# A hand-written instruction list with the same 848 entries in another order: attention overlapped with the first pass of a feed-forward layer

## The chip, the cores and the metric

The kernel runs on one core of one Trainium2 chip. The metric is device time in microseconds (us), the median of several runs. Matmuls run on TensorE (PE; its weight loads are PEld), and element work on VectorE (DVE), ScalarE (ACT) and GpSimd (POOL). All transfers of this kernel are issued by SyncE (SP). Each engine takes its instructions strictly in the order in which the program gives them to it, and semaphores hold an instruction until its operands are there.

## The reference

Three stages, one after the other. Batch is 2, heads are 8, the sequence is 768, the head dimension is 64.

1. Attention: each query sees the keys nearer than 16 positions, and also 24 block summaries (per block of 32 keys the elementwise maximum of the keys and the mean of the values, with log 32 added to their scores). Softmax over both sets together.
2. First feed-forward layer on the 1536 x 512 result x: `h = max(x @ w_in, 0)`, `x = (h * h) @ w_out`, with a hidden size of 2048.
3. Second layer of the same shape: a rational function of `h = x @ w_in` (a cubic over a quadratic in |h|), then `@ w_out`.

Inputs of the two layers come as 64-bit floats and are decoded on the chip.

## The kernel before, in words

Matmuls of the two layers are each done as three: a number is split into a high and a low part, and high x high, high x low and low x high are summed. The layers are run in four passes over parts of the 16 tiles of the hidden size (128 columns each). Pass 0 does tiles 0 to 4 of the first layer, in six chunks of 256 tokens: 30 steps, one for each chunk and tile. Pass 1 does the other 11 tiles, passes 2 and 3 the second layer.

Pass 0 is interwoven with the attention. The attention is cut into 24 units d (six groups of 256 queries, four pairs of heads); units 4c to 4c+3 give the tokens of chunk c. The order of all instructions of this stage is written out by hand, as one string `ORDER` of 848 entries. The program walks through it and calls a function for each entry; each engine gets its instructions in the order of the entries. A scheduler orders only what follows the list, from step 28 of pass 0 on.

An entry is a letter and a number:

- SP, transfers: `E` keys of batch 0 (a pair of heads), `q_1`, `q_0` and `Q` queries of a group, `v`, `Z` values for the block means, `N` windows of values, `J` keys of batch 1, `I` raw weights of one half tile (3 buffers, so a load waits until the decoding of the one three before has read its buffer).
- Keys: `P` (POOL) rearranges them, `t` (DVE clears two PSUM banks, PE transposes), `l` and `k` copy the two banks to SBUF, `c` (DVE) takes the block maxima and writes them for some windows, `B` for the rest.
- Block means of values: `S` (POOL) adds, `V` (PE) sums up, `u` and `w` copy out.
- A unit d of attention: `q` (PE transposes queries), `z` (ACT copies them), `s` (PE scores, 4 matmuls that the trace shows as 8), `m` (DVE adds the mask and takes the maximum, 4 instructions), `e` (ACT exponential, 4), `r` (DVE sum and reciprocal, 2), `n` (POOL scales, 4), `p` (PE transposes, 4), `b` (copies), `o` (PE times values), `x` (ACT) and `y` (DVE) split the result into its high and low part.
- Weights of one half tile: `T` (ACT), `D` (DVE, 2 instructions), `W` (ACT), `M` (POOL).
- Pass 0, step g: `h(4g)` to `h(4g+3)` (PE, 3 matmuls each, the first layer's product), `i` (ACT) and `j` (DVE) square the positive part, `G` (ACT) and `H` (POOL) split it, `Y(4g)` to `Y(4g+3)` (PE, 3 matmuls each, the second product).
- `_z0`, `_m2`, `_bw` and the like set up constants.

A star sends a copy (`l`, `k`, `B`, `u`, `w`, `b`) to DVE, without one it runs on ACT:

```python
            elif x[-1] == "*":
                parts[x[0]](int(x[1:-1]), dve)
            else:
                parts[x[0]](int(x[1:]))
```

The attention has six PSUM banks, `y0` to `y3`, `a0` and `a1`. Each user takes the one that came free earliest in the list and gives it back in the entry that reads it last:

```python
        tag = banks.pop(0)
```

From the entry `O0` on, `y0` and `y1` are kept for the sums of pass 0: the first step's `Y0` and `Y1` go into `y0`, and `Y2` and `Y3` into `y1`.

Of the kernel before, what the change touches and what calls it, by code (L numbers as in the profile page):

```python
# [16 lines left out]


ORDER = (
    "E0 _id P0 E1 q_1 t0 P1 q_0 _m0 t1 q2 q1 l0 _z0 E2 _m1 k0 k1* q3 P2 I0 E3 l1 z1 q0 c1 _pr s1 "  # L20
    "_ml z0 P3 t2 c0 _m2 k2 Q1 l2 T0 _bw s0 m0 e0 z2 c2 t3 m1 q6 l3* D0 k3 v0 B1 S0 e1 r0 n0 s2 "
    "c3 B2 W0 q4 v1 m2 S1 z3 s3 I1 q5 p0 e2 r1 V0 r2 B0 N0 m3 n1 z5 z4 s4 T1 u0 w0 p1 b0* e3 D1 "
    "M0 b1* v3 s5 n2 m4 v2 q7 p2 N1 z6 o0 o1 S2 e4 S3 I2 W1 N3 x1 r3 z7 x0 N2 b2* m5 B3* T2 n3 V1 "
    "p3 r4 s6 M1 I3 b3 Q2 u1* w1 m6 I4 y0 D2 N4 o2 N5 e5 r5 n4 T3 o3 y1 x2 h0 p4 y2 x3 I5 D3 s7 "
    "h1 W2 I6 y3 h2 n5 p5 e6 W3 q9 r6 q8 m7 M2 z9 q10 h3 z8 T4 h4 J1 J3 h5 h6 b5* b4* q11 e7 i0 "
    "D4 W4 h7 n6 i1 M3 s8 p6 m8 J2 j0 z10 o5 o4 r7 I7 s9 M4 G0 h8 x5 T5 h9 z11 x4 m9 b6* D5 H0 O0 "
    "y4 Y0 Y1 Y2 h10 n7 h11 T6 D6 j1 s10 e8 W6 W5 i2 Y3 y5 p7 J0 t5 r8 I8 N6 M6 h12 G1 H1 h13 e9 "
    "Y4 h14 m10 M5 k5* b7 n8 Y5 Y6 N7 j2 N8 h15 e10 i3 l5* r9 Y7 s11 p8 r10 N9 G2 T7 t4 T8 k4 D7 "
    "H2 Y8 D8 n10 W7 n9 W8 Z0 Y9 I9 J5 m11 Y10 M8 o6 Y11 o7 b8 o8 x6 N11 h16 h17 x7 j3 h18 J4 e11 "
    "h19 y6 y7 l4 r11 M7 c5 i4 h20 h21 h22 G3 h23 H3 p10 Y12 Y13 x8 Y14 y8 I10 i5 j4 p9 T9 b9* j5 "  # L30
    "D9 Y15 h24 G4 I11 h25 h26 h27 o9 S4 W9 M9 h28 H4 h29 i6 h30 b10* V2 h31 G5 t6 Y16 H5 Y17 j6 "
    "Y18 Y19 h32 Y20 Z1 i7 Y21 G6 k6 c4 Y22 Y23 H6 x9 Y24 Y25 Y26 T10 h33 h34 Q3 h35 n11 J7 T11 "
    "j7 u2* D10 D11 N10 i8 Y27 h36 h37 h38 j8 G7 l6* H7 W10 h39 i9 G8 M10 Y28 Y29 Y30 W11 h40 Y31 "
    "H8 j9 Y32 Y33 p11 y9 I12 q12 Y34 Y35 b11 z12 o11 x11 o10 J6 h41 I13 s12 x10 T12 y10 y11 m12 "
    "h42 h43 h44 i10 M11 h45 S5 h46 j10 G9 h47 H9 i11 N13 T13 t7 Y36 D12 G10 Y37 Y38 Y39 h48 H10 "
    "W12 e12 D13 Y40 I14 Y41 Y42 M12 q13 Q4 w2 z13 h49 h50 r12 h51 j11 k7* Y43 h52 i12 c6 G11 T14 "
    "H11 s13 W13 Y44 Y45 m13 Y46 I15 Y47 h53 e13 q14 j12 h54 h55 n12 z14 i13 G12 D14 M13 H12 h56 "
    "q15 s14 h57 l7* r13 m14 Y48 Y49 z15 Y50 N15 h58 W14 j13 e14 c7 h59 M14 p12 B4 r14 i14 G13 "
    "b12* T15 I16 n13 Y51 s15 V3 m15 e15 j14 B5* H13 u3 Y52 r15 p13 T16 Y53 Y54 b13 B7* n14 N12 "
    "B6* N14 n15 o12 p14 x12 w3* y12 o13 x13 b14* p15 Y55 b15 D15 o14 y13 x14 o15 x15 h60 Q5 y14 "  # L40
    "h61 y15 h62 h63 W15 q16 D16 M15 h64 h65 h66 i15 G14 H14 j15 h67 i16 G15 Y56 Y57 Y58 h68 j16 "
    "H15 Y59 z16 Y60 h69 h70 h71 i17 I17 Y61 Y62 G16 Y63 H16 W16 q17 s16 Y64 Y65 m16 e16 N18 Y66 "
    "z17 Y67 h72 N17 h73 j17 s17 r16 m17 q19 h74 M16 e17 h75 h76 z19 h77 i18 n16 q18 G17 p16 s19 "
    "z18 r17 m19 e19 H17 Y68 Y69 T17 Y70 Y71 j18 s18 N16 n17 h78 r19 b16 m18 q20 D17 h79 o16 e18 "
    "z20 i19 n19 G18 p19 r18 p17 W17 H18 b17* x16 s20 Y72 Y73 y16 n18 o17 x17 Y74 Y75 p18 b19 m20 "
    "b18 N19 q21 z21 y17 o19 h80 j19 x19 o18 x18 e20 M17 y19 s21 h81 y18 h82 h83 q22 i20 j20 h84 "
    "G19 h85 H19 h86 r20 h87 m21 i21 G20 H20 Y76 Y77 n20 Y78 Y79 h88 Y80 h89 Y81 h90 z22 h91 Y82 "
    "N20 j21 e21 Y83 h92 i22 h93 q23 G21 H21 N23 r21 N22 Y84 N21 Y85 h94 h95 z23 j22 Y86 i23 Y87 "
    "s22 G22 H22 p20 Y88 Y89 n21 m22 b20* Y90 e22 s23 r22 m23 Y91 h96 n22 j23 h97 h98 p21 e23 b21 "
    "h99 i24 G23 o20 r23 o21 n23 p23 x20 H23 p22 y20 Y92 x21 b23* Y93 y21 b22 j24 Y94 o22 x22 y22 "  # L50
    "Y95 o23 h100 h101 x23 y23 h102 h103 i25 j25 G24 h104 h105 h106 H24 h107 h108 i26 Y96 Y97 Y98 "
    "G25 Y99 h109 h110 h111 H25 Y100 Y101 j26 i27 Y102 j27 G26 Y103 H26 h112 Y104 h113 Y105 Y106 "
    "h114 h115 i28 h116 j28 G27 H27 h117 h118 h119 Y107 i29 j29 Y108 Y109 G28 Y110 H28 Y111 "
)


# [795 lines left out]
```

## Time and profile before

| | us |
|---|---|
| median of 3 runs (lowest, highest) | 629.76 (628.51, 630.88) |
| the profiled execution, its own time | 628.86 |
| the profiled execution, its span | 626.8 |
| last matmul of the list (`Y111`) starts | 175.73 |

The span is the time from the first to the last instruction that the profile shows; the execution's own time is 2.06 us more. The list takes the first 176 us, and the rest of the span is passes 1 to 3. A matmul's row shows its start, so that the distance between two starts is its cost in a dense stretch.

### The profile page before, as it was taken

What the parts mean: (1) busy time and instruction counts of PE and PEld (TensorE: products, weight loads), DVE (VectorE), ACT (ScalarE), POOL (GpSimd) and SP (SyncE); (2) the same over time, 40 slices, a digit from 0 to 9 for tenths busy, and PEclk for the clock granted to TensorE, in tenths of its full rate; (3) what the DMA queues carried; (4) which work ended last, traced back from release to release, by engine and by line L of the source; (5) the groups of instructions that cost most, each with busy time, mean ns of one, the idle gap of its engine ahead of it and who ended that gap; (6) DMA issues with size and microseconds to landing.
All of it is one profiled execution on the core that took longest, in us unless ns stands there. A gap on an engine that the chain in (4) does not pass through costs nothing.

```text
span 626.8 us, 9738 instructions
## 1 busy us (share of the span) xinstructions
PE 604.4 (96%) x3488; PEld 517.4 (83%) x3488; DVE 407.4 (65%) x811; ACT 402.6 (64%) x770; POOL 353.6 (56%) x363
## 2 busy tenths in 40 slices
PE   5798999999999999999999999999999999999997
PEld 5788898989988778888888888788888888888886
DVE  3988659565347674011137799988666977776673
ACT  3888558575355554122256899988878788877761
POOL 3677876444246775222277799954545764544451
PEclk9899999999999999999999999999999999999999
DMA  9978795411025553000006433410000100001011
GB/s 222 260 176 199 176 240 144 118 47 40 3 68 168 183 157 98 0 1 0 1 0 195 155 122 100 135 35 1 1 0 1 34 1 1 1 19 49 0 68 67
DMA packets 64143, 51.48 MB, mean 82 GB/s; under 512 B 39776, under 2 KB 56160, under 8 KB 64096
## 3 DMA queue, kind: packets, MB, share of 16 engines
q1 hardware_dynamic: 64096, 50.87, 29.9%
q8 instruction: 27, 0.44, 0.3%
q14 instruction: 20, 0.16, 0.1%
HBM read 47.71 MB, written 3.15 MB: 81 GB/s over the span
## 4 chain that ended last, share of the span: by engine, by line
PE 50%; DVE 7%; ACT 2%; POOL 2%; issue 1%; DMA 1%; POOLq 0%; ACTq 0%; SPq 0%; DVEq 0%
PE y L665 25%; PE h L571 25%; DVE wdec L160 2%; POOL wl L176 2%; ACT wdec L149 1%; POOL sl L641 1%; DVE acc L693 1%; DVE h L620 1%; DVE q L617 1%; DVE wdec L159 1%; DVE p L605 1%; DVE p L623 1%; DVE p L604 1%; DMA wraw<-in_moe_w_out_dram 1%; ACT sh L634 1%
## 5 line engine op out<-in xcount | busy, mean ns | idle before, releaser
L571 PE MATMUL h<-xh,wh 128*128 128x512 f32 (+1 forms) x444 | 162.4, 366 | 1.2 <-DVE r L601 0.8
L571 PE MATMUL h<-xh,wl 128*128 128x512 f32 (+1 forms) x444 | 160.1, 361 | 0.8 <-POOL wl L176 0.8
L571 PE MATMUL h<-xl,wh 128*128 128x512 f32 (+1 forms) x444 | 160.1, 361 | 0.2 <-DVE xl L539 0.2
L641 POOL TENSOR_TENSOR sl<-r,sh 128x512 fp32r<-128x512 f32 (+1 forms) x63 | 67.9, 1078 | 116.3 <-ACT sh L634 94.6
L592 POOL TENSOR_TENSOR q<-q,u 128x512 f32<-128x512 f32 x48 | 63.6, 1326 | 76.3 <-ACT q L589 74.0
L176 POOL TENSOR_TENSOR wl<-wdec,wh 128x512 fp32r<-128x512 f32 x64 | 87.5, 1374 | 25.0 <-ACT wh L171 25.0
L571 PEld LDWEIGHTS h<-xh,wh 128*128 128x128 f32 x444 | 83.6, 188 | 15.2 <-DVE p L623 1.2
L571 PEld LDWEIGHTS h<-xh,wl 128*128 128x128 f32 x444 | 83.7, 189 | 13.5 <-POOL wl L176 1.0
L571 PEld LDWEIGHTS h<-xl,wh 128*128 128x128 f32 x444 | 83.8, 189 | 12.9 <-DVE xl L539 0.4
L601 DVE TENSOR_TENSOR r<-r,h 128x512 f32<-128x512 f32 (+1 forms) x63 | 35.1, 557 | 85.5 <-ACT r L584 85.4
L665 PE MATMUL y<-sh,wh 128*128 128x512 f32 (+1 forms) x252 | 87.3, 347 | 3.4 <-DVE xl L539 1.8
L665 PE MATMUL y<-sh,wl 128*128 128x512 f32 (+1 forms) x252 | 85.1, 338 | 0.0
L665 PE MATMUL y<-sl,wh 128*128 128x512 f32 (+1 forms) x252 | 81.1, 342 | 0.6 <-POOL sl L641 0.6
L641 POOL TENSOR_TENSOR sl<-p,sh 128x512 fp32r<-128x512 f32 x48 | 64.8, 1351 | 20.4 <-ACT sh L634 17.0
L665 PE MATMUL y<-wl,sh 128*128 128x512 f32 x192 | 74.7, 389 | 0.0
L665 PE MATMUL y<-wh,sh 128*128 128x512 f32 x192 | 74.4, 389 | 0.0
L665 PE MATMUL y<-wh,sl 128*128 128x512 f32 x192 | 74.0, 389 | 0.0
L160 DVE SCALAR_TENSOR_TENSOR wdec<-wraw,wdec 128x512 int32<-128x512 int32 x64 | 68.5, 1071 | 1.7
L584 ACT ACTIVATE r<-h 128x512 f32<-128x512 f32 (+1 forms) x63 | 31.1, 494 | 47.0 <-PE h L571 25.7
L171 ACT CAST wh<-wdec 128x512 fp32r<-128x512 f32 x64 | 39.5, 620 | 33.4 <-DVE wdec L160 31.3
L634 ACT CAST sh<-r 128x512 fp32r<-128x512 f32 (+1 forms) x63 | 32.3, 513 | 39.1 <-PE y L665 38.6
L159 DVE TENSOR_SCALAR wdec<-wdec 128x512 int32<-128x512 int32 x64 | 45.9, 718 | 17.2 <-ACT wdec L149 17.0
(88 smaller groups left out, 1094.3 us busy)
## 6 DMA issues: line engine op xcount, KB each, us to landing
wraw<-in_moe_w_in_dram SPq DMA_DIRECT2D x32, 512.0 KB, 4.0
wraw<-in_moe_w_out_dram SPq DMA_DIRECT2D x32, 512.0 KB, 3.4
early<-in_v_dram SPq DMA_DIRECT2D x40, 96.0 KB, 3.8
out_dram<-acc SPq DMA_DIRECT2D x12, 256.0 KB, 2.1
acc<-in_q_dram SPq DMA_DIRECT2D x10, 256.0 KB, 6.8
early<-in_k_dram SPq DMA_DIRECT2D x4, 384.0 KB, 5.5
early<-in_v_dram SPq DMA_DIRECT2D x4, 384.0 KB, 7.8
kst<-in_k_dram SPq DMA_DIRECT2D x8, 192.0 KB, 5.3
```

Source lines behind the costliest of these rows:

```text
L149: x = nc.scalar.activation(out=f32(t), in_=f32(r[:, :, 1]), func=AF.Prelu, scale=2.0 ** -112, alpha=-(2.0 ** 32))
L159: nc.vector.tensor_single_scalar(out=t, in_=t, scalar=3, op=ALU.logical_shift_left)
L160: nc.vector.scalar_tensor_tensor(out=t, in0=low, scalar=29, in1=t, op0=ALU.logical_shift_right, op1=ALU.bitwise_or)
L171: nc.scalar.copy(out=wt[n][0][:, j], in_=f32(wdec[n, j]))
L176: nc.gpsimd.tensor_tensor(out=tl[:, j], in0=t, in1=f32(th[:, j]), op=ALU.subtract)
L571: nc.tensor.matmul(hq[g][:, 0:n], lhsT=w[:, 0, ws], rhs=x[:, part, ts], start=(part == 0 and j == 0), stop=(part == KC - 1 and j == 2),)
L584: nc.scalar.activation(out=r, in_=h, func=AF.Relu)
L592: nc.gpsimd.tensor_tensor(out=q_, in0=q_, in1=u_, op=ALU.mult)
L601: nc.vector.tensor_tensor(out=eq[g], in0=eq[g], in1=h, op=ALU.mult)
L634: nc.scalar.copy(out=sh[:, 0:n], in_=e)
L641: nc.gpsimd.tensor_tensor(out=sl[:, 0:n], in0=eq.pop(g), in1=f32(sh[:, 0:n]), op=ALU.subtract)
L665: x = nc.tensor.matmul(o, lhsT=lt, rhs=rt, start=(f == 0 and j == 0 and d * m % 512 == 0), stop=(f == FS[ps] - 1 and j == 2 and (d + 1) * ...
```

## The change

The string `ORDER` is replaced by one with the same 848 entries in another order. Nothing is added or taken away, except that 21 entries change their star: `l0`, `k6`, `B1`, `B2`, `B4`, `u0`, `w2`, `b7`, `b8` and `b13` move from ACT to DVE, and `k1`, `k5`, `k7`, `l3`, `l6`, `B5`, `u2`, `w3`, `b0`, `b12` and `b23` from DVE to ACT. No other line of the program is changed. The beginning of both lists, up to the first step of pass 0, and some of what the prediction speaks of:

```diff
 ORDER = (
-    "E0 _id P0 E1 q_1 t0 P1 q_0 _m0 t1 q2 q1 l0 _z0 E2 _m1 k0 k1* q3 P2 I0 E3 l1 z1 q0 c1 _pr s1 "
-    "_ml z0 P3 t2 c0 _m2 k2 Q1 l2 T0 _bw s0 m0 e0 z2 c2 t3 m1 q6 l3* D0 k3 v0 B1 S0 e1 r0 n0 s2 "
-    "c3 B2 W0 q4 v1 m2 S1 z3 s3 I1 q5 p0 e2 r1 V0 r2 B0 N0 m3 n1 z5 z4 s4 T1 u0 w0 p1 b0* e3 D1 "
-    "M0 b1* v3 s5 n2 m4 v2 q7 p2 N1 z6 o0 o1 S2 e4 S3 I2 W1 N3 x1 r3 z7 x0 N2 b2* m5 B3* T2 n3 V1 "
-    "p3 r4 s6 M1 I3 b3 Q2 u1* w1 m6 I4 y0 D2 N4 o2 N5 e5 r5 n4 T3 o3 y1 x2 h0 p4 y2 x3 I5 D3 s7 "
-    "h1 W2 I6 y3 h2 n5 p5 e6 W3 q9 r6 q8 m7 M2 z9 q10 h3 z8 T4 h4 J1 J3 h5 h6 b5* b4* q11 e7 i0 "
-    "D4 W4 h7 n6 i1 M3 s8 p6 m8 J2 j0 z10 o5 o4 r7 I7 s9 M4 G0 h8 x5 T5 h9 z11 x4 m9 b6* D5 H0 O0 "
-    "y4 Y0 Y1 Y2 h10 n7 h11 T6 D6 j1 s10 e8 W6 W5 i2 Y3 y5 p7 J0 t5 r8 I8 N6 M6 h12 G1 H1 h13 e9 "
...
+    "E0 _id E1 E2 P0 q_0 _m0 _pr t0 P1 k0 t1 _m1 _z0 _ml P2 l1 k1 E3 l0* q_1 _bw Q1 q0 z0 q1 c0 "
+    "t2 z1 _m2 l2 s0 P3 q3 k2 B0 c1 t3 m0 e0 q2 c2 l3 z2 r0 k3 n0 s1 q7 m1 q4 I0 v0 c3 s2 v1 q5 "
+    "N1 z3 e1 s3 v3 S0 m2 r1 p0 e2 m3 r2 T0 N0 e3 S1 B2* V0 v2 n1 z4 B1* b0 D0 q6 u0* z5 s4 w0 p1 "
+    "m4 o0 e4 r3 I1 I2 s5 z6 n2 Q2 p2 b1* B3* N2 T1 o1 m5 W0 r4 z7 x0 x1 S2 n3 s6 p3 D1 M0 I3 N3 "
+    "e5 y0 S3 I4 y1 W1 m6 n4 h0 b2* T2 e6 V1 r5 D2 q9 h1 s7 u1* q8 p4 w1 M1 b3 N5 W2 T3 z8 N4 o3 "
+    "o2 n5 x2 s8 x3 r6 D3 I5 y2 h2 y3 h3 M2 W3 q10 h4 T4 m7 D4 b4* e7 h5 n6 h6 I6 q11 W4 i0 J2 p5 "
+    "h7 b5* M3 o4 o5 z9 j0 p6 M4 i1 m8 r7 I7 G0 b6* O0 h8 x4 z10 T5 H0 h9 j1 Y0 D5 Y1 n7 T6 x5 "
+    "h10 h11 Y2 s9 N6 J3 i2 G1 W5 J1 J0 Y3 z11 D6 N7 y5 H1 m9 y4 M5 W6 Y4 Y5 Y6 I8 M6 s10 e8 t5 "
+    "N8 p7 h12 h13 T7 h14 j2 r8 m10 b7* h15 Y7 N9 k5 e10 i3 G2 Z0 t4 D7 l4 T8 I9 o6 n8 p8 H2 x6 "
+    "k4 r10 Y8 J5 D8 b8* J4 Y9 W7 Y10 W8 Y11 n10 y6 o7 M8 o8 e9 s11 h16 h17 x8 h18 I10 j3 x7 h19 "
...
 )
```

## Rows read from the trace of the kernel before

**Rows 1.** The page, busy time and share of the span: TensorE

```profile
PE 604.4 (96%) x3488; PEld 517.4 (83%) x3488; DVE 407.4 (65%) x811; ACT 402.6 (64%) x770; POOL 353.6 (56%) x363
```

**Rows 2.** Windows: stretch, length, busy us (instructions) by engine, granted clock, DMA share, GB/s

```profile
core 0: us, PE busy (x) PEld busy (x) DVE busy (x) ACT busy (x) POOL busy (x), PEclk, DMA share, GB/s
0.00:26.00 26.00, 15.76 (x90) 14.54 (x91) 15.28 (x69) 14.17 (x35) 10.77 (x26) 0.93 1.05 241
26.00:44.00 18.00, 17.00 (x184) 15.54 (x183) 16.07 (x65) 16.72 (x47) 15.61 (x27) 1.00 0.86 198
44.00:66.00 22.00, 19.15 (x216) 17.93 (x214) 19.18 (x69) 17.98 (x49) 15.70 (x25) 1.00 0.89 197
66.00:110.00 44.00, 42.37 (x396) 40.73 (x394) 31.93 (x92) 27.97 (x73) 32.10 (x47) 1.00 0.77 182
110.00:176.00 66.00, 65.00 (x644) 61.58 (x645) 32.85 (x121) 36.95 (x104) 26.95 (x53) 1.00 0.19 49
176.00:626.80 450.80, 445.08 (x1970) 367.04 (x1968) 292.05 (x398) 288.79 (x467) 252.51 (x189) 1.00 0.18 58
```

**Rows 3.** Timeline of the first 25 us: start, us, engine, line, operation, [idle before <-releaser]

```profile
4.68 1.03 POOL L303 COPY early<-early 96x1024 f32<-96x1024 f32 x1 [3.24 <-DMA early<-in_k_dram]
5.77 3.18 PE L371 MATMUL pk<-ident,early 96*128 96x96 f32 x16 [5.77 <-POOL early L303]
6.31 1.04 POOL L303 COPY early<-early 96x1024 f32<-96x1024 f32 x1 [0.60 <-DMA early<-in_k_dram]
...
8.74 1.91 PE L436 MATMUL pt<-ident,acc 128*128 128x128 f32 x8
...
9.84 1.61 ACT L444 COPY qz<-pt 64x256 f32<-64x256 f32 x4 [0.85 <-PE pt L436]
9.85 0.95 DVE L391 TENSOR_REDUCE kss<-kt 128x24 f32<-128x768 f32 x1
10.16 1.04 POOL L303 COPY early<-early 96x1024 f32<-96x1024 f32 x1 [2.27 <-DMA early<-in_k_dram]
...
11.41 2.04 PE L455 MATMUL pss<-kt,qz 128*128 128x120 f32 x8 [0.76 <-DVE kt L397]
...
13.27 1.04 POOL L303 COPY early<-early 96x1024 f32<-96x1024 f32 x1 [2.07 <-DMA early<-in_k_dram]
...
14.52 1.72 PE L455 MATMUL pss<-kt,qz 128*128 128x120 f32 x8
...
16.27 0.28 DVE L470 CUSTOM_DVE_ANT_0 pr<-pss,mask 128x120 f32<-128x120 f32 x1 [2.44 <-PE pss L455]
...
18.85 1.15 PE L371 MATMUL pk<-ident,early 96*128 96x96 f32 x8 [2.61 <-DVE pk L368]
...
23.55 1.15 PE L455 MATMUL pss<-kt,qz 128*128 128x120 f32 x8 [1.01 <-DVE mx L470]
```

**Rows 4.** Windows around the low clock, columns as in the first windows

```profile
16.00:20.00 4.00, 1.39 (x12) 1.23 (x11) 3.69 (x21) 2.38 (x7) 1.26 (x1) 0.91 1.10 283
20.00:23.00 3.00, 2.54 (x12) 2.14 (x11) 2.90 (x7) 2.97 (x9) 0.79 (x3) 0.55 1.07 250
```

**Rows 5.** Lines of the list's stretch: busy, mean ns of one | idle before

```profile
L479 ACT ACTIVATE pr<-pr,mx 128x120 f32<-128x120 f32 x96 | 30.1, 386 | 7.8 <-DVE mx L470 7.6
L470 DVE CUSTOM_DVE_ANT_0 pr<-pss,mask 128x120 f32<-128x120 f32 x96 | 21.2, 277 | 13.5 <-PE pss L455 12.2 <-POOL pr L494 1.1 <-PE ptp L504 0.2
L487 DVE TENSOR_REDUCE mx<-pr 128x4 f32<-128x484 f32 x24 | 15.6, 649 | 3.8 <-ACT pr L479 3.6
L160 DVE SCALAR_TENSOR_TENSOR wdec<-wraw,wdec 128x512 int32<-128x512 int32 x18 | 14.0, 777 | 0.6
```

**Rows 6.** Timeline at two waits of TensorE after 44 us

```profile
50.13 0.41 DVE L539 TENSOR_TENSOR xl<-pav,xh 128x256 fp32r<-128x256 f32 x1
...
50.69 0.35 PE L665 MATMUL y<-sh,wh 128*128 128x256 f32 x1 [1.75 <-DVE xl L539]
...
63.87 0.38 PE L571 MATMUL h<-xh,wl 128*128 128x256 f32 x1 [0.77 <-POOL wl L176]
```

51 rows, old and new, of the table ORDER are left out of this document.

## Prediction

> **What bounds the kernel now.** I read the page's busy times first, then windows over the list's stretch, then the timeline of the start, then the timeline at the longest waits that were left. TensorE (PE) is busy for 96% of the span [rows 1], so the time can only fall where PE waits or runs slowly. The windows say where [rows 2]: after 176 us PE is busy 445.08 of 450.80 us and runs code that the change doesn't touch; before, it has 26.00 - 15.76 = 10.24 us without work in the first 26 us, then 1.00, 2.85, 1.63 and 1.00. That is 16.7 us, and 5.77 of them come before the first keys are there and rearranged [rows 3]; 10.95 are within reach of an order. The granted clock adds to it: eight score matmuls took 2.04 us at the start and 1.15 once warm [rows 3].
>
> Within the list three kinds of stretch follow each other. Up to 16.27 us everything waits for transfers and for the first scores: the first mask instruction (`m0`) stands at 16.27, and right after it PE idles 2.61 us, because `t3` stands behind other DVE work [rows 3]. From 26 to 66 us DVE is busy 35.25 of 40 us and ACT 34.70 [rows 2]; PE's waits there are handed down from them. After 66 us DVE and ACT have a quarter or more of the time free, and PE is the bound. So a lead won early is kept if the other engines can follow, and lost if a transfer or a bank can't.
>
> **The change, part by part.** Work is not added or removed: the new list has the same entries, and 21 copies change between ACT and DVE, ten one way and eleven the other. By the lists' counts ACT gets about one copy more and DVE one less in 176 us of which both are busy less than 70%; I cost this at nothing over the stretch, at most one `k` or `l` copy (under 1 us) in the busy part, either way.
>
> *The start.* Two key loads of 384 KB reach their readers at 4.68 and 6.31 us, so 1.63 us each while the queue is full. As a check, the third comes 512 KB of queries later: 1.63 x 896/384 = 3.80, and its reader starts 3.85 us after the second [rows 3]. In the new list `E2` comes third on SP's queue and one half of the queries (`q_0`, 256 KB) fourth: landed at 7.94 and 9.03; `E3` fifth, at 10.66, in place of 13.27. POOL's `P2` runs 7.94 to 8.98. PE's order is now t0 t1 q0 q1 t2 s0: t1 is through at 8.74 as before, `q0` and `q1` wait for the queries until 9.03 and take half of the 1.91 us of four such units, to 9.99; `t2` at the low clock takes about half of the 3.18 us of the first two less the wait between them, 1.35, to 11.34; `s0` takes 16.27 - 14.52 = 1.75, to 13.1 [rows 3]. DVE has by then done `l0`, `c0`, the masks and most of `c1` (the maxima, 0.95 us each [rows 3]), and ACT `z0` (a quarter of 1.61 for each copy, done near 10.4). So `m0` starts at 13.1 in place of 16.27: **-3.2 us**. `t3` (keys at 10.66, rearranged at 11.7) follows `s0` and `q3` at 13.5 in place of 18.85, and the 2.61 us of idle PE are gone; what they cost stands in this 3.2 or in the next term, and isn't counted again.
>
> *Straight after it.* DVE's next waits in the new order are for scores: `s1` stands behind s0, q3, t3 and q2 on PE (0.48 + 1.35 + 0.48), ends near 17.1, while DVE is through with `c2` and `r0` near 16. **+1.0 us** of the lead is given back; the bounds are 0 (if the clock has risen by then, `s1` takes 1.15) and 2.
>
> *Between 26 and 44 us.* DVE idles 18 - 16.07 = 1.93 us there [rows 2]. Following the new list entry by entry I find it nearly without waits: `D0` to `D3` (0.64 + 0.78 us or a little more each, by the rows' L160 with its partner) stand later among the units, so `r6` has three of them ahead and no longer four, and the inputs of each `m` (0.28 x 4 less overlap) and `r` (0.65 and a reciprocal) are there when DVE comes [rows 5]. `e` on ACT, 0.39 x 4 less overlap [rows 5], is in the same position. The bounds are 0 and 1.93; I take three quarters, **-1.4 us**, since the first products of the layer (`h0`) still wait for `M0`, whose `W0` now stands later (ACT does `W0` after `e4` and not after `e1`). By my reading `h0` starts near 30.6 with less PE work ahead of it, and PE idles there some 1.5 us, which is priced in.
>
> *The bank of Y2.* In the old list `y1` was held by unit 4 (`o4`) when `O0` reserved it, so that `Y2` waited for `y4`, which stood behind `D5` on DVE: PE idled 1.75 us until 50.69, the last read being at 50.13 to 50.54 [rows 6]. Counting banks through the new list, `y1` is held by `q10` and given back by `z10` on ACT, which stands before `T5`; `y0` was last read by `m8`. By the time of `Y2` both are free: **-1.75 us**. If `z10` were late, 0.
>
> *The weights of h16.* The third matmul of `h16` waited 0.77 us for `M8` on POOL [rows 6]. In the new list `M8` goes before `M7` as it did, but `n9` comes after both, and `h16` stands behind o7, o8 and s11. I reckon the wait gone or halved: **-0.5 us** (0 to -0.77).
>
> *After 66 us.* PE idles 2.63 us in 110 us [rows 2]. The distances on PE between a unit's scores, its transposes and its use are about the same in both lists (units 16 to 19 have more, 21 and 22 less), so I expect the same small waits: 0, with 1.5 either way.
>
> *After the list.* The entries left are the same and the weights are equally far (18 half tiles). The rest moves up as a block; the scheduler sees another start, which I cost at 0, 1 either way.
>
> The sum is -3.2 + 1.0 - 1.4 - 1.75 - 0.5 = -5.85 us. Against the profiled execution's own 628.86 us (span 626.8 and 2.06 around it) that is 623.0. The median of the three runs, 629.76, lies 0.9 above that execution, so I put the predicted time at 623.6.
>
> **A rule weighed.** After PE had idled up to 18.85 us, the granted clock was 0.55 in 20 to 23 us [rows 4] and back at 1.00 from 26 on [rows 2]: the lower of the two levels (1.2 and 2.4 GHz) after little work. The Trainium skill (TensorE: Matmul & The Clock Gate, "HAM oscillation — how this bites in real kernels") says that a PE that keeps waiting between short bursts falls back to half speed again and again. The trace agrees for that one stretch. By the rows alone the new order takes away the long idle but leaves PE sparse between 17 and 31 us, as it runs ahead of DVE; my sum takes one such stretch in it as free, since DVE and ACT have the work there. What it would be otherwise is the second rival.
>
> **The rivals.** *Transfers become the bound.* A kernel that is 6 us ahead needs its transfers 6 us earlier. I count 14.4 MB in the new queue up to `I10`, with `J4` and `J5` for `t6` ahead of it; at the 241 GB/s of the first 26 us [rows 2] they are there at 60 us, about 4 us before I expect `t6` to want its keys. At the 197 GB/s of 44 to 66 us they come at 73 us, and nearly all of the lead goes. For it: the DMA share there is already 0.89. Against it: SP waited for free buffers in that stretch, so 197 is demand as much as limit. It gives some -1.3 us, 627.6 to 630: no change.
>
> *The clock stays low*, the case on the other side. PE is busy 17.00 us in 26 to 44 us at the full clock [rows 2]; the rows at both levels give a factor 2.04/1.15 = 1.77 [rows 3]. If the new order's sparse PE holds the low level through the like stretch, it needs 30 us there, 12 more than the 18, and the time becomes 623.6 + 12 = 635.6. Each us of that work at the low level costs 0.77 once the 1.0 us of idle is used up, so it turns the sign from about 9 us of low clock on. The skill's rule named above speaks for it; against it, the `s` at 23.55 us in the old order runs at full speed after 1.01 us of idle [rows 3].
>
> *The change does little:* the early lead is eaten by local waits in chunks 3 to 5. PE idled only 2.63 us there, but a different set of waits of 0.5 us for each of twelve units would take 6 us back: 629.6.
>
> **How the numbers follow.** No change means within 0.5% (3.1 us), about what a measurement of this kernel can tell. I give the forecast, a lead of 3.2 us or more that lasts, 0.67; the two that end without a change (transfers, later waits) 0.21 together; slower, by the clock or by a queue whose waits I read wrongly, 0.12. The lower end is 10 us under the median, 619.5, with all bounds taken well (-3.2, 0, -1.93, -1.75, -0.77, -1.5, -1); the idle of 10.95 us forbids much more. The upper end takes in the first and third rivals: 630.5.
>
> **What would show it.** In the new profile: `P2` near 8 and the third key load's reader no longer at 10.16; the first mask instruction near 13.1; no PE wait of 2.6 us before `t3`; no wait of PE on `y4` before `Y2`; the third matmul of `h16` before 59 and not at 63.87; the list's last matmul near 170. It is wrong if PE's waits for `z` or `m` grow between 17 and 31 us with the clock at 0.5 beyond 31, if SP's transfers land after their readers are ready near `t6`, or if PE's idle between 66 and 170 us is several us more than 2.63.

## The result and the profile after

The new list takes 620.00 us (median of 4, 619.52 to 620.75) against 630.32 beside it (4, 628.51 to 630.94): a ratio of 0.985, 95% interval 0.983 to 0.988. The forecast was 623.6 within 619.5 to 630.5, so the sign is right, the time lies at the low end of the range, and the gain is larger than the sum of its terms. The profiled execution took 620.43 us with a span of 618.5, so 8.3 us less of span than before. That difference is what has to be found in the trace. The other 2 us between the medians have no trace: the kernel before took 626.5 to 632.3 us over all its executions beside these runs, and the profiled one took 628.86.

The page's busy line, which answers to [rows 1]:

```profile
PE 600.2 (97%) x3488; PEld 515.6 (83%) x3488; DVE 407.6 (66%) x810; ACT 403.2 (65%) x771; POOL 356.4 (58%) x363
```

TensorE is busy for 4.2 us less with the same 3488 matmuls. Its "busy" time therefore holds more than the work, waits or matmuls at the lower clock, and that will matter below. The windows that answer to [rows 2]:

```profile
core 0: us, PE busy (x) PEld busy (x) DVE busy (x) ACT busy (x) POOL busy (x), PEclk, DMA share, GB/s
0.00:26.00 26.00, 18.09 (x136) 16.38 (x137) 18.99 (x88) 17.89 (x45) 14.42 (x32) 1.00 1.06 242
26.00:44.00 18.00, 14.56 (x147) 13.24 (x147) 16.13 (x49) 13.53 (x37) 13.71 (x22) 0.91 0.79 196
44.00:66.00 22.00, 21.71 (x240) 20.75 (x237) 19.11 (x68) 18.46 (x50) 18.75 (x27) 1.00 1.10 224
66.00:110.00 44.00, 43.61 (x446) 42.33 (x446) 33.38 (x96) 30.11 (x80) 30.38 (x47) 1.00 0.67 153
110.00:176.00 66.00, 65.73 (x615) 63.35 (x614) 33.83 (x121) 38.97 (x106) 29.74 (x54) 1.00 0.27 69
```

The first row is better by 2.33 us of busy PE and by the clock (1.00, before 0.93). The second is worse: PE idles 3.44 us (before 1.00) at a clock of 0.91. The third is better by 2.56.

A second measure shows what the windows don't. For each entry of the list I take its start on PE before, minus its start after, and correct for the PE work that stands ahead of it in one list and not in the other (each entry at its cost in a dense stretch, so `h` and `Y` at 3 x 0.12, and `V1` with its 16 matmuls at 1.75). That is the lead of PE at that entry. An entry's start is that of its first matmul; for `Y111` the table of the time before gives the second, 175.73. The experiments below are in the same table:

```
entry  start before  lead: new  new,old  old,new  new+u1*  start only
s6        33.91         +4.24   +4.39    +0.85    +4.10     +0.12
h4        41.68         +0.71   +0.43    +0.85    +2.36     +0.12
Y0        47.95         +0.90   +0.48    +0.86    +2.41     -0.43
Y2        50.69         +2.92   +2.49    +0.87    +4.43     +1.52
h16       62.59         +2.31   +1.96    +0.88    +3.91     +0.81
h20       65.16         +3.36   +3.01    +0.87    +4.95     +0.80
h32       75.63         +3.33   +1.50    +0.53    +4.79     +0.82
h48       92.40         +3.55   +1.52    +0.85    +4.97     +0.84
h60      112.84         +5.63   +1.70    +2.97    +7.05     +1.03
h80      139.15         +7.66   +1.72    +5.01    +9.08     +1.04
Y111     175.61         +8.75   +1.76    +6.10   +10.19     +0.81
```

In the new list 4.2 us are won by `s6`, 3.5 of them are gone again by `h4`, 2 come back at `Y2`, and 5.4 are won after `h20`. After `Y111` 0.45 is lost. Two executions of the same beginning differ by up to 1.4 us in their first 17 us (a column that starts with the old order shows +0.85), so only changes along a column are read.

The start, as in [rows 3], from the timeline:

```profile
7.50 1.03 POOL L304 COPY early<-early 96x1024 f32<-96x1024 f32 x1
...
10.75 1.96 PE L456 MATMUL pss<-kt,qz 128*128 128x120 f32 x8
...
12.74 0.28 DVE L471 CUSTOM_DVE_ANT_0 pr<-pss,mask 128x120 f32<-128x120 f32 x1 [1.16 <-PE pss L456]
12.93 0.85 PE L372 MATMUL pk<-ident,early 96*128 96x96 f32 x8
...
13.83 1.05 PE L456 MATMUL pss<-kt,qz 128*128 128x120 f32 x8
```

The third rearrangement of keys is at 7.50 (10.16 before), the first mask instruction at 12.74 (16.27), `t3` runs at 12.93 without a wait (18.85 after 2.61), and `s1` takes 1.05 us, at the full clock already. Where the lead goes stands between 32 and 39 us (in the new list's own profiles a line has a number one higher than in the others, so L160 and L161 here are L159 and L160 there):

```profile
32.54 1.27 POOL L177 TENSOR_TENSOR wl<-wdec,wh 128x512 fp32r<-128x512 f32 x1
...
32.84 1.26 DVE L160 TENSOR_SCALAR wdec<-wdec 128x512 int32<-128x512 int32 x1
...
34.13 0.74 DVE L161 SCALAR_TENSOR_TENSOR wdec<-wraw,wdec 128x512 int32<-128x512 int32 x1
...
34.90 0.78 DVE L419 COPY early<-pvs 24x256 f32<-24x256 f32 x2
...
35.76 0.63 ACT L419 COPY early<-pvs 24x256 f32<-24x256 f32 x2 [2.90 <-DVE early L419]
...
37.05 1.97 PE L521 MATMUL pav<-pp,early 120*64 120x64 f32 x32 [2.22 <-ACT pp L509]
```

On DVE `u1*` stands behind `D2` (L160 and L161), which lasts from 32.84 to 34.87. `w1` on ACT waits 2.90 us for `u1*`, `b3` stands behind `w1` on ACT, and `o3` on PE waits 2.22 us for `b3`. The granted clock is then 0.64 in 36 to 39 us, partly at the lower of its two levels.

### The profile page after: what moved, and what is told of

It reads as the page before. It is cut to its first block, busy times and chain, and to the rows that moved or that the text cites. A ratio compares the mean times of both kernels' runs of the same rounds, so it can differ in the third digit from the quotient of the medians.

```text
span 618.5 us, 9770 instructions
## 1 busy us (share of the span) xinstructions
PE 600.2 (97%) x3488; PEld 515.6 (83%) x3488; DVE 407.6 (66%) x810; ACT 403.2 (65%) x771; POOL 356.4 (58%) x363
## 4 chain that ended last, share of the span: by engine, by line
PE 50%; DVE 7%; POOL 3%; ACT 2%; issue 1%; POOLq 0%; ACTq 0%; DVEq 0%
PE y L666 25%; PE h L572 25%; DVE wdec L161 2%; POOL wl L177 2%; POOL sl L642 1%; DVE acc L694 1%; DVE h L621 1%; ACT wdec L150 1%; DVE wdec L160 1%; DVE q L618 1%; DVE p L624 1%; DVE p L606 1%; DVE p L605 1%; ACT sh L635 0%; ACT wh L172 0%
## 5 line engine op out<-in xcount | busy, mean ns | idle before, releaser
L161 DVE SCALAR_TENSOR_TENSOR wdec<-wraw,wdec 128x512 int32<-128x512 int32 x64 | 68.7, 1073 | 1.7
L160 DVE TENSOR_SCALAR wdec<-wdec 128x512 int32<-128x512 int32 x64 | 46.4, 726 | 20.7 <-ACT wdec L150 20.6
```

Source lines behind the costliest of these rows:

```text
L160: nc.vector.tensor_single_scalar(out=t, in_=t, scalar=3, op=ALU.logical_shift_left)
L161: nc.vector.scalar_tensor_tensor(out=t, in0=low, scalar=29, in1=t, op0=ALU.logical_shift_right, op1=ALU.bitwise_or)
```

## The experiments

All kernels keep the 848 entries and change only their order; a part that is taken from a list keeps that list's stars. No run changes the stars alone. Ratios are to the kernel before on the same chip.

**Two halves.** The new list up to `h20` and the remaining entries in the old order, and the other way round:

```diff
-... y7 l4 r11 M7 c5 i4 h20 h21 h22 G3 ...
+... j3 x7 h19 i4 G3 r9 h20 l5* n9 m11 N11 e11 y7 ...
```


> The new list up to its entry h20 (the first product of the second chunk), then all entries that are left in the order of the old list. Theory A (each part of the order is worth the waits that it takes away, and leads add up): the new list leads by 3.4 us at h20, so the span falls from 626.8 to about 623.4, the last matmul of the list from 175.6 to about 172.2. Rival B (the later gain of 5.4 us is a consequence of the early lead, since the other engines and the transfers are further ahead): the span falls to about 619 to 620. Rival C (the old tail absorbs the lead): 626 to 627.

> The old list up to its entry h20, then all entries that are left in the order of the new list. Theory A: the later part of the new order is worth 5.4 us by itself, so the span is about 621.4 and the last matmul of the list starts near 170.2. Rival B (the later gain needs the early lead): 625 to 627.

New then old: 626.88 us, ratio 0.996 (0.994 to 0.998). Old then new: 623.63, ratio 0.991 (0.988 to 0.993). The spans are 1.9 and 6.1 us shorter than before, together 8.0 of the 8.3. The two halves add up to within 0.3 us, though the first span, 624.9, lies between theory A and rival C. The second half needs no lead: in the table its column gains 5.2 us after `h20` with nothing won before. The first keeps 1.5 us of its 3.0, the rest is lost at the seam, where `h24` waits 1.3 us for an `r` on DVE.

**The early part alone.** The new list up to `o0`, then the old order:

```diff
-... u0 w0 p1 b0* e3 D1 M0 b1* v3 s5 ...
+... u0* z5 s4 w0 p1 m4 o0 W0 I1 T1 D1 M0 b1* s5 ...
```


> The new list up to its entry o0 (24 us), then all entries that are left in the order of the old list. Theory A: the lead of 4.5 us that the new order has at o0 is kept by the old order, since its own u1* and w1 don't hold each other up; the old bank of Y2 and the old late waits come back. Span about 622.5 to 623.5. Rival B (in 26 to 44 us DVE and ACT set the pace, so that most of the lead of TensorE at o0 is one of order and not of time): 624.5 to 626.

629.15 us beside 629.08: ratio 1.002 (1.000 to 1.004). Theory A fell; the span of the profiled execution, 625.7, lies in the rival's range, but that execution was the fastest of the twelve. A lead of 4.83 us at `o0` is 0.12 at `s6`. It went through a transfer: the old order decodes the second half tile (`T1`, `D1`) at once, and the new beginning has loaded it late, as the timeline shows.

```profile
26.52 0.67 ACT L149 ACTIVATE wdec<-wraw 128x512 f32<-128x512 f32 x1 [1.45 <-DMA wraw<-in_moe_w_out_dram]
...
27.22 0.50 DVE L159 TENSOR_SCALAR wdec<-wdec 128x512 int32<-128x512 int32 x1 [2.59 <-ACT wdec L149]
```

TensorE then waits 0.92 us in `p2` and 0.91 in `o1`, and `V1` takes 3.24 us in place of 1.75, with a granted clock of 0.54 in 30 to 33 us. So ahead of the old order the early lead is worth nothing. That it is the later place of the decoding that lets the new list keep some of it is not shown by itself. This is the nearest that any run comes to the rival of the transfers; in the new list's own two profiles no wait for one of over 0.3 us shows after 26 us, and in the other profiles with its beginning ACT waits up to 0.87 us for one near 27 us. With the changes below that give a greater lead, ACT also waits for weights at 66 to 70 us, 0.84 us in one profile and up to 1.72 in another, without a loss on PE (in the second, a lead of 4.86 at `h20` and 4.82 at `h32`).

**The wait of w1.** The new list with `u1*` ahead of `D2`:

```diff
-... V1 r5 D2 q9 h1 s7 u1* q8 p4 w1 ...
+... V1 r5 u1* D2 q9 h1 s7 q8 p4 w1 ...
```


> The new list with the one entry u1* moved ahead of D2 on DVE. In the new kernel w1 on ACT waits 2.9 us for u1*, which stands behind D2, and TensorE then waits 2.2 us for the copy b3 and runs at the low clock after it. Theory A: about 2 us of the lead of 4.7 us that the new order has at h0 is lost there; with u1* ahead of D2 the wait of ACT falls below 1.5 us, the clock stays up, and the span falls from 618.5 to about 616.5 (615.5 to 617.5). Rival C: DVE is the bound in that stretch, so that the order on it changes nothing: 618 to 619.

618.67 us, ratio 0.983 (0.980 to 0.985). The timeline:

```profile
33.09 0.77 DVE L418 COPY early<-pvs 24x256 f32<-24x256 f32 x2
...
33.95 0.64 ACT L418 COPY early<-pvs 24x256 f32<-24x256 f32 x2 [0.97 <-DVE early L418]
...
35.24 0.98 PE L520 MATMUL pav<-pp,early 120*64 120x64 f32 x26 [0.27 <-ACT pp L508]
```

`w1` waits 0.97 in place of 2.90, `o3` 0.27 in place of 2.22, and the clock stays at 1.00 in 36 to 39 us. At `h4` the lead is 2.36, not 0.71, and it is kept to the end (10.19). So the wait of `w1` behind `D2` was 1.4 to 1.65 us of the loss.

**The bank of Y2.** The old list with `y4` ahead of `D5`:

```diff
-... b6* D5 H0 O0 y4 Y0 Y1 Y2 ...
+... b6* y4 D5 H0 O0 Y0 Y1 Y2 ...
```


> The old list with the one entry y4 moved ahead of D5 on DVE, so that the bank of Y2 comes free some 1.3 us earlier. Theory A: TensorE's wait of 1.75 us before Y2 falls to about 0.5, and the span from 626.8 to about 625.6. Rival C: the wait moves to the next one (h12 waits for the weights that D5 and D6 make) and the span stays at 626.5 to 627.

628.05 us, ratio 0.998 (0.996 to 0.999), so 1.6 us less by the medians, while the profiled execution's span is 626.8 as before. PE's wait falls from 1.75 to 1.0 us. The lead rises by 0.77 at `Y2`, and 0.36 of it is left at `h20`. The wait was real; less than half of it is won by this move alone, the whole by the new list, in which `z10` has given the bank back before.

**The waits after 66 us.** The old list with `j11` ahead of `D13`, and then with three more moves, each of an entry that a wait of PE names:

```diff
-... W12 e12 D13 Y40 ... h51 j11 k7* ...
+... W12 e12 j11 D13 Y40 ... h51 k7* ...
```


> The old list with the one entry j11 moved ahead of D13 on DVE. In the old kernel the matmul h52 waits 0.85 us for j11, whose PSUM buffer it takes over and which stands behind D13 and r12 (95.28 to 96.44). Theory A (behind 66 us every small wait of TensorE counts in full, and the later gain is a sum of such waits): the wait goes, and the last matmul of the list and the span come about 1.0 us earlier, 625.8 by the span of the old profile. Rival C (the next entry in the queue waits instead): 626.5 to 627.


```diff
-... r15 p13 T16 Y53 Y54 b13 ... h77 i18 n16 q18 G17 ... z20 i19 n19 G18 ...
+... r15 p13 b13 T16 Y53 Y54 ... h77 G17 i18 n16 q18 ... z20 G18 i19 n19 ...
```


> The old list with four entries moved a little ahead of their neighbours, each on an engine on which TensorE waits for it after 90 us: j11 ahead of D13 (DVE), b13 ahead of T16 (ACT), G17 ahead of i18 and G18 ahead of i19 (ACT). Theory A (the later gain is a sum of small waits that count in full): 1.0 as before, 0.5 for the wait of o13 on b13, and 0.4 each for Y68 and Y72, whose H17 and H18 follow G17 and G18; the last matmul of the list comes 2.0 to 2.3 us earlier against the same point at 90 us, and the span is about 624.5. Rival C (a wait that is taken away comes back at the next entry): no more than the 0.9 us of j11 alone, 625.9.

628.37 us, ratio 1.000 (0.997 to 1.002), and 628.21, ratio 0.997 (0.995 to 0.999). One move is too small for the time to tell; in the trace the wait before `h52`, in the kernel before

```profile
96.50 0.38 PE L571 MATMUL h<-xh,wh 128*128 128x256 f32 x1 [0.85 <-DVE r L601]
```

is gone, which wins 1.0 us at `h52` and keeps 0.8. The four together win 1.4 of the 2.0 to 2.3 that their waits add up to: `j11` 0.8 to 1.0, `b13` 0.4, and `G17` and `G18` 0.2 together. These two win 0.3 at `Y68` and 0.5 at `Y72`, but 0.5 is lost between them, where `p19` now waits 0.31 us for `n19`: the four POOL instructions of `n19` take 1.99 us in place of 1.55, with all of `D17` on DVE beside them. So each of the old order's four late waits can be taken away by where an entry stands, and most of what is won is kept, but not all: the last part comes back at another entry, as rival C has it. The span of the profiled execution, 625.9, is that rival's number.

**One move too many.** `u1*` ahead of `D2`, and also `j5` ahead of `D9`:

```diff
-... H3 ... Y13 Y14 G4 D9 Y15 h24 N11 e11 h25 y8 j5 W9 ...
+... H3 ... Y13 Y14 G4 j5 D9 Y15 h24 N11 e11 h25 y8 W9 ...
```


> The new list with u1* ahead of D2 as before, and also j5 moved ahead of D9 on DVE: in that kernel h28 waits for j5, whose buffer it takes over, behind D9 of 2.2 us (TensorE loses 0.6 us at 65 us). Theory A: the 0.6 us are kept to the end, the span falls from 616.3 to about 615.7. Rival C: the 0.6 us come back at the next wait for DVE (b9* for o9, or D9's weights), 616 to 616.5.

621.46 us, ratio 0.986 (0.983 to 0.989): about 3 us more than without the move of `j5` (618.67), where a little less was expected. The trace lost its lead at two places, and one of them lies ahead of the move. I therefore ran both again, with the new list as it is, on one chip:

> The new list with u1* ahead of D2 once more, on the chip on which the next two kernels run. Its first run took 618.67 us, and the kernel with one move more (j5 ahead of D9) 621.46. The profile of that one loses 5 us of lead between 27 and 36 us, where the two lists are still the same, and 3.5 us between 73 and 84 us, where one DVE instruction of the decoding took 2.71 us while POOL worked beside it. Theory S (the lists are equal, and a DVE instruction that happens to lie beside POOL work is stretched in some executions): this kernel 617.5 to 621 and within 1.5 us of the next one. Rival J (the move of j5 is harmful): this kernel 618.7 as before, and the next one 2 us or more above it.

> The new list with u1* ahead of D2 and j5 ahead of D9 once more, on the same chip. Theory S: within 1.5 us of the kernel before it, and a profile in which the decoding of D1 or D9 is not stretched has the last matmul of the list near 165.5. Rival J: 621 to 622, with a wait of TensorE between 73 and 84 us again.

> The new list as it is, on the same chip as the two with u1* moved. If moving u1* is worth what its first profile showed (1.44 us of lead at the end of the list), this one is 1 to 2 us slower than that kernel, 619.5 to 620.5. If the spread of the beginnings hides that, the two are equal within 1 us.

| kernel | us (lowest, highest) | ratio, interval |
|---|---|---|
| new list | 620.11 (619.66, 621.09) | 0.986 (0.984, 0.989) |
| with `u1*` ahead of `D2` | 618.26 (618.11, 618.93) | 0.983 (0.980, 0.986) |
| with `j5` ahead of `D9` too | 622.41 (621.26, 623.81) | 0.990 (0.987, 0.992) |

The theory that the last two are equal fell: moving `j5` costs. The gain of `u1*`, 1.85 us, is there again, and the two sets of times don't overlap. What moving `j5` does is in the timeline of its second run:

```profile
73.04 2.06 POOL L494 TENSOR_SCALAR pr<-pr,rs 128x120 f32<-128x120 f32 x4
...
74.91 2.70 DVE L160 SCALAR_TENSOR_TENSOR wdec<-wraw,wdec 128x512 int32<-128x512 int32 x1
...
75.08 0.73 POOL L641 TENSOR_TENSOR sl<-r,sh 128x256 fp32r<-128x256 f32 x1
...
75.78 1.28 POOL L176 TENSOR_TENSOR wl<-wdec,wh 128x512 fp32r<-128x512 f32 x1
```

The second instruction of `D11` begins while POOL works, POOL goes from one instruction to the next without a gap until 77.06, and the DVE instruction ends at 77.61, 0.55 us after that. It takes 2.70 us where 0.69 is the rule; in the kernel without the move it took 1.11. PE waits 1.85 us for the `r` behind it (L601), and 2 us of lead are gone between `h32` and `h40`. Of the 4.1 us by which this execution ends its list later than that of `u1*` alone, these 2 are the move's; the other 2.2 are lost by `h4`, at `D1`, where the two lists are still the same.

The other loss, at `D1`, is the same pattern, and it doesn't depend on the list: of the two profiles of the new list itself, one has it and ends with a lead of 7.66 us, the other, in the table, has not and ends with 8.75. The timeline of the kernel with `u1*` alone (second run):

```profile
28.86 0.40 DVE L159 TENSOR_SCALAR wdec<-wdec 128x512 int32<-128x512 int32 x1
...
28.98 1.40 POOL L176 TENSOR_TENSOR wl<-wdec,wh 128x512 fp32r<-128x512 f32 x1 [0.38 <-ACT wh L171]
29.29 1.64 DVE L160 SCALAR_TENSOR_TENSOR wdec<-wraw,wdec 128x512 int32<-128x512 int32 x1
...
31.32 0.39 PE L571 MATMUL h<-xl,wh 128*128 128x256 f32 x1 [0.83 <-DVE xl L539]
```

and of the kernel with `j5` moved (second run), the list being the same up to here:

```profile
28.25 1.26 POOL L176 TENSOR_TENSOR wl<-wdec,wh 128x512 fp32r<-128x512 f32 x1
...
28.53 1.26 DVE L159 TENSOR_SCALAR wdec<-wdec 128x512 int32<-128x512 int32 x1
...
29.83 1.79 DVE L160 SCALAR_TENSOR_TENSOR wdec<-wraw,wdec 128x512 int32<-128x512 int32 x1
...
32.01 0.58 PE L571 MATMUL h<-xl,wh 128*128 128x256 f32 x1 [2.38 <-DVE xl L539]
```

In seven profiles with this beginning the first instruction of `D1` took 0.40 us in four and 1.26 to 1.49 in three. In three of the four it began 0.12 or 0.13 us before `M0` (in the fourth `M0`'s row begins 0.04 earlier, and there `M0` took 1.56). In the other three `M0` began first, by 0.05 to 0.28 us, and the instruction ended 0.28 or 0.29 us after `M0`. PE's longest wait in `h0` was 0.82 to 0.99 us in the four of the first kind and 2.25 to 2.38 in the second, with a granted clock of 0.50 in 33 to 36 us in the run shown, but of 1.00 in the second profile of the new list, where the wait was 2.25. What decides which comes first is not shown; the two starts shift by tenths of a us between executions.

**D1 out of POOL's way.** `u1*` ahead of `D2`, and `D1` ahead of `r4`:

```diff
-... o1 m5 W0 r4 z7 x0 x1 S2 n3 s6 p3 D1 M0 ...
+... o1 m5 W0 D1 r4 z7 x0 x1 S2 n3 s6 p3 M0 ...
```


> The new list with u1* ahead of D2 and D1 ahead of r4. In seven profiles with this beginning D1's first instruction took 0.40 us where it began before POOL's M0, and 1.26 to 1.49 us where M0 began first; the second instruction took 1.64 to 1.79 us each time. Theory (DVE and POOL hold something that only one has at a time, for a whole instruction): D1 now begins about half a us ahead of M0, so its two instructions take 0.40 and 0.69 to 0.8 us, M0 is late or long instead, TensorE's second matmul of h0 waits 0.4 us or less in place of 0.83 to 2.38, and the time is 617 to 618.5, within 0.5% of the kernel with u1* alone (618.26 and 618.67). Rival (DVE is slowed by whatever POOL does beside it, whoever began first): the second instruction still takes 1.6 us or more.

618.49 us (617.80 to 620.47), ratio 0.983 (0.981 to 0.987). The timeline:

```profile
27.82 0.43 DVE L159 TENSOR_SCALAR wdec<-wdec 128x512 int32<-128x512 int32 x1
...
28.29 0.73 DVE L160 SCALAR_TENSOR_TENSOR wdec<-wraw,wdec 128x512 int32<-128x512 int32 x1
28.45 1.70 POOL L176 TENSOR_TENSOR wl<-wdec,wh 128x512 fp32r<-128x512 f32 x1
...
30.16 0.39 PE L571 MATMUL h<-xl,wh 128*128 128x256 f32 x1 [0.28 <-DVE xl L539]
```

Begun first, `D1` takes 0.43 and 0.73 us, and now it is POOL's `M0` that takes 1.70 in place of 1.26 to 1.56. That shows which of the two pays: the one that comes second. The wait in `h0` is 0.28 us. The time is that of the kernel with `u1*` alone: the 0.5 us won at `h0` is not to be seen at `h4` (2.35 against 2.36). The next wait takes it back:

```profile
35.41 0.62 ACT L171 CAST wh<-wdec 128x512 fp32r<-128x512 f32 x1 [0.65 <-DVE wdec L160]
...
37.28 0.93 PE L455 MATMUL pss<-kt,qz 128*128 128x120 f32 x6 [1.18 <-ACT qz L444]
```

`s8` waits 1.18 us for `z8` (0.89 with `u1*` alone) and starts at 37.28 in both kernels. `z8` stands behind `W2` on ACT, and `W2` waits for `D2`, which now comes after `u1*`. The version with `u1*` ahead of `D2` is the one that beats both kernels, by 1.3 to 1.9 us against the new list.

## Why the prediction was right or wrong

**The start: right.** The term was -3.2 us, and the first mask instruction came 3.5 us earlier, by the transfers worked out (`P2` at 7.50, forecast 7.94 to 8.98). The +1.0 that was to follow it didn't come, since the clock had risen by `s1` (1.05 us, one of the bounds named). By `s6` the lead is 4.2, where the terms had 2.2. But the start is not worth that by itself: alone, it left the time as it was.

**26 to 44 us: this step failed.** It had a gain of 1.4 us with bounds of 0 and 1.93; the runs show a loss of 3.5. Following the entries I costed `D0` to `D3` at 0.64 + 0.78 us "or a little more", from means such as that of [rows 5]. `D2` took 2.03, because its first instruction met POOL's `M1`. I also did not ask who waits for `u1*` behind it: `w1`, then `b3`, then `o3`. Moving `u1*` gave 1.65 us of it back. Of the rest the traces name the wait of `h0` for `y0` behind `D1` (0.82 us) and, once `u1*` is moved, that of `s8` for `z8` (0.89); the last run took 0.5 off the first and saw 0.3 come back at the second, so the order on ACT and DVE up to `z8` is the likely rest, which no run settles.

**The bank of Y2: right.** -1.75 was forecast; the lead rises by 2.0 from `Y0` to `Y2`, and moving `y4` in the old list showed that the wait was what the trace said. **The weights of h16:** -0.5 was forecast, 1.05 is won from `h16` to `h20`, after 0.6 lost since `Y2`; the third matmul of `h16` came at 60.60 without a wait, but not before 59.

**After 66 us: the term of 0 ± 1.5 was mis-sized; it is -5.4.** I expected "the same small waits" because PE idled only 2.63 us there, and I took the idle time as the most that an order can give (also where the range's lower end says that "the idle of 10.95 us forbids much more"). The view of PE's waits in 66 to 176 us before,

```profile
PE h L571 <- DVE r L601: 0.8, 1, 0.8
PE y L665 <- POOL sl L641: 0.6, 3, 0.2
PE pav L520 <- ACT pp L508: 0.5, 1, 0.5
```

and after,

```profile
PE h L572 <- DVE r L602: 0.4, 1, 0.4
PE ptp L505 <- POOL pr L495: 0.3, 1, 0.3
```

is the same in kind, and the waits before are hardly larger. The distances between the starts tell more. A matmul's row is 0.28 us long, and in a dense stretch the next begins 0.12 us later: up to 0.16 us of each wait lies under the row of the matmul before it and counts as busy. The time that PE's entries take beyond their dense cost, from 66 us to the end of the list, is 8.33 us before and 2.94 after, a difference of 5.4 (the two sums move together by some 2 us with what is taken as dense, the difference doesn't); ten places of 0.31 to 1.01 us are 5.6 of it before, and three are 1.5 after, so that these make 4.1 of the difference and smaller ones 1.3. Some 0.7 of the small ones, by an estimate from the usual distances, are no waits: an entry's cost depends on what follows it (an `h` costs 0.36 us before another and 0.45 to 0.53 before an `o`), and after `h20` the new list changes the kind of entry on PE 117 times, the old one 131 times. That this is the order, and not the lead, is shown by the run of old then new (5.2 us with no lead). That it is these waits is shown for 1.4 us of it, by the four moves; for the rest it is argued from the distances. The stars were not tested apart from the order: `b13`, for which `o13` waits 0.5 us before, stands on DVE in the new list.

**After the list:** 0 was forecast, 0.45 is lost.

The terms measured along the lead are -4.2, +3.3 (to `Y0`), -2.0, +0.6, -1.05, -5.4 and +0.45, in sum -8.3 us. The forecast of -5.85 comes that near because two misses cancel, 4.7 us too much hoped for in 26 to 44 us and 5.4 us not seen after 66: that the time fell into the range is in part luck. The list's last matmul starts at 167.10, forecast near 170. (The forecast's own sum, 623.0 and 0.9, is 623.9 and not 623.6.)

**The rivals.** The transfers did not become the bound in the new list. The clock fell to 0.64, but only near 36 to 39 us and behind the wait of 2.22 us, and it cost no lead: in the profile of the new list up to `h20` `o3` waits 2.21 us, the clock stays at 1.00, and the lead at `h4` is 0.43, no more than the 0.71 here. The Trainium skill's section named in the prediction (TensorE: Matmul & The Clock Gate, "HAM oscillation — how this bites in real kernels") tells of a clock that falls again and again. Within the list, it fell once in one of the new list's two profiles, behind that wait, and not at all in the other. Local waits did eat most of the early lead (3.5 of 4.2 us), as the third rival has it, but between 26 and 44 us and not in chunks 3 to 5; there the new order won.

## What to carry to other kernels

Read what an order can give from the distances between the starts of matmuls against their dense distance, not from the idle time: here 5.4 us were won in a stretch that showed 2.63 us of idle. An instruction that others wait for goes ahead of a long one on its engine, and the chain behind it is followed across engines until it reaches the bound (`u1*`, `w1`, `b3`, `o3`). Where VectorE and GpSimd both work, cost an instruction with what the other one does at its start, and judge a list by several executions: two profiles of the same one ended their lists 1.1 us apart. When a wait is taken away, look for the next one on the other engines before counting the gain (`h0`, then `s8`).

## What the runs showed of the hardware

A VectorE instruction of the decoding that begins while GpSimd runs a two-input operation does not slow down in proportion: it ends a fixed time after GpSimd's. The first instruction (L159, a shift) took 0.40 to 0.43 us alone, and where it was stretched it mostly ended 0.28 to 0.34 us after the GpSimd row; the second (L160, a shift and an or of two tensors) took 0.69 alone, and stretched it ended 0.55 or 0.56 after it in 50 of 53 places in the list's stretch of all the traces, and in both executions with `j5` moved after a run of GpSimd work without a gap (2.70 and 2.71 us). Begun first, VectorE kept its 0.40, and `M0` on GpSimd took 1.39 to 1.70 in place of 1.26.

The Trainium skill (SBUF — State Buffer, "SBUF: two separate sides") says that VectorE, with an instruction in a mode of two ports or with two inputs in SBUF, and GpSimd share a pair of ports, which the one that begins first holds for its whole instruction while the other is blocked. The runs agree, with the numbers above, but the start of a row is not a sure sign of who holds them: in one profile `M0`'s row began 0.04 us earlier and VectorE still kept its 0.40, and in the 2.70 us case two GpSimd instructions whose rows began 0.17 and 0.87 us after VectorE's went ahead of it.
